# A long convolution by a two-stage Fourier transform: 2048 steps as 64 by 32 instead of 128 by 16, with half-array matmuls in the first and last stage

## The chip, the cores and the metric

One core of one Trainium2 chip. The metric is the device time of one execution in microseconds (us), over several executions; the profile is of one execution. A core has TensorE (PE; its weight loads are listed apart as PEld), VectorE (DVE), ScalarE (ACT), GpSimd (POOL) and SyncE (SP), each working through its own instructions in order, and 16 DMA engines which they start transfers on.

## The reference

Two branches over the same 2048 x 640 input `x`, joined at the end (bf16 inputs):

```python
x = A_q                                   # [1, 2048, 640]
xn = layernorm(x)
# branch A: q = xn
k_shift = sum(k_pad[:, t:t+S, :] * shift_k[:, 3-t] for t in range(4))
kv = k_shift * v
y = irfft(rfft(pad(kv, 2S)) * rfft(pad(ssm_k, 2S)))[:S]   # along the 2048 steps, per channel
s = xn * (y + kv * ssm_D)
# branch B
g = silu(gelu(xn @ w1 + b1) @ w2 + b2)    # 640 -> 1728 -> 640
out = x + s * g
```

## The kernel before

**The transform.** The convolution is done with real matmuls. The 2048 steps are numbered 16 p + j, with p = 0..127 on the partitions and j = 0..15 along the free axis (`NJ = 16`). The first stage contracts over the 128 partitions, for each j on its own: `k_f1` for the filter and `u_f1` for the gated input kv multiply a 128x128 matrix of cosines (`WA[:, j]`) and one of sines (`WB[:, j]`) with the 640 channels, in two halves of 320 (`HALF`). So one j is four matmuls of 128x128 weights with 320 columns, through `mm2` (L337). The results, of 128 lines each, are copied out of PSUM to bf16 (`evac`, ScalarE L135 or VectorE L136), stored to DRAM scratch (`k_store` L437, `u_store` L447, by GpSimd) and loaded again in another order by SyncE (`kin_load` L477, `uin_load` L513), which transposes between stages. The second stage (`k_f2`, `u_f2`) is one small 128x128 matrix for every group of lines. Its products with the filter's transform (`product`, L526 on VectorE) go through a first inverse stage (`inv1`, L534 and L535), again to scratch (`c_store` L541) and back (`cab_load` L547). The last stage `inv2` (L553, L554) adds, for each j, a cosine and a sine part: four matmuls of 128x128 weights (`GA`, `GB`) with 320 columns. `gate` (L560, VectorE) multiplies the result y with the rest, `out_add` (L564) adds x, and `out_store` (L568, GpSimd) or `last_store` (L416, SyncE) writes the output.

**Where the matrices come from.** `WA` and `WB` are made in the kernel: an integer product of step and frequency (L231 on VectorE, masked at L235), then three passes on ScalarE of 128x2048 (sine L239, absolute value L242, sine L244). `GA` and `GB` are their transposes, made on TensorE (`i2_tr` L488, 32 transposes in four steps it0 to it3). The filter comes with channels on the partitions, so it is transposed too: `k_tr` (L421), five 128x128 transposes per j.

**The second branch** is `ffn1` (L377, h: 128x512 matmuls, Gelu at L383) and `ffn2` (L396, g: groups of fourteen 128x320 matmuls, Silu at L401, product L406). The transposes of xn for it are tt (L368).

**PSUM** has a pool `big` of three buffers of two banks, for all of the transform, and a pool `ffn` of two buffers. A matmul that needs a buffer waits until its last user has read it.

**What sets the order.** A list written out by hand, `PLAN`, gives the order of all steps; the instructions of each engine stand in that order. A step such as `kf5` is one call of `k_f1(5)`, `ke5.a` copies its result out on ScalarE (`.d`: VectorE), `kt`, `kc` are the transposes of the filter and their copies, `uf`, `ue`, `us` the first stage of kv and its copies and stores, `y`, `yt`, `yo`, `ys` the last stage, its gate, add and store, `it`, `ie` the transposes of the matrices. The loads (`load_x` L168, `load_k` L173 to L175, `load_v` L179, `load_params` L187 to L191, `load_w1` L195, `xq_load` L544) are issued by SyncE in the order of the list. The first Gelu needs the bias b1, which is loaded by `load_params` and transposed on TensorE (`param_tr`, L505, 19 partitions).

Of the kernel before, what the change touches and what calls it, by code (L numbers as in the profile page):

```python
# [16 lines left out]
P = 128  # L17
# [16 lines left out]
ln7 ln5 ws2 C4 C3 C1 V0 cv7 cv15 C2 d kt0 kc0.a kt1 kc1.a kf0 kf1 ke0.a kt2 kc2.a V1 ln4 kf2 ke2.a cv24 cv23 X2  # L34
cv25 ke1.d ks0 gm2 ge4 ln6 kf3 ke3.d ks1 kf4 ke4.a gm4 ge5 kt3 kc3.d kf5 ke5.a ks2 V2 tt7 te7.a kt5 kc5.d tt9
te9.a kt4 gm5 kf7 cv26 cv27 cv28 kf6 kc4.a ke6.a ke7.a ks3 g6 ge6 kf8 ke8.a kf9 ke9.d ks4 kf10 ke10.a K2 tt8
te8.a kt6 kc6.d kf11 ke11.a ks5 kt9 kc9.d gm3 kf12 ke12.a tt5 te5.d tt6 te6.a uf1 kt7 kf13 kc7.a ke13.a ks6 g7
ge7 ls12 uf0 ue0.a ue1.d us0 cv29 cv30 cv31 V3 h14 he14 kf14 ke14.d kf15 ke15.d ks7 h15 he15 kt8 kc8.d kf19 kf18
ke18.a ke19.d ks9 kt10 kc10.a cv32 cv33 cv34 cv35 cv36 kf16 ke16.a kt12 cv40 kf17 kc12.a ke17.a ks8 h16 he16 uf3
uf2 ue2.a ue3.a us1 h17 he17 kf21 kf20 ke20.a ke21.d ks10 kt11 kc11.a h18 he18 uf5 uf4 ue4.a ue5.d us2 kf22  # L40
ke22.d ls10 h19 he19 kt14 kf24 ke24.d sm kf23 kc14.a ke23.a ks11 h20 he20 kf25 ke25.d ks12 kt13 kc13.d kf28
ke28.a h21 he21 uf6 ue6.a kf29 ke29.a ks14 uf7 ue7.a us3 h22 he22 h23 he23 kf26 ke26.a gm7 cv37 cv38 cv41 cv42
cv39 kf27 ke27.a ks13 kt15 kc15.d kf30 ke30.a kf31 ke31.a ks15 fl0 fl1 fl2 h24 he24 fl4 uf10 ue10.a gm6 ls15 ls8
ls9 uf8 ue8.a ls14 uf11 ue11.a us5 h25 he25 h26 he26 uf14 ue14.a cv43 ls13 lv3 lr3 h27 he27 cv44 ls11 lv2 lr2
cv45 cv46 cv47 uf12 ue12.a uf9 ue9.a us4 fl3 uf15 ue15.a us7 g8 ge8 gm8 ln13 ln9 uf13 ue13.a us6 fl5 g9 ge9 ff3
fe3.a ln12 ff1 fe1.d ln10 ff2 fe2.a cv56 ff0 fe0.a cv48 cv49 cv50 ln8 uf21 uf20 ue20.a ue21.a us10 ff8 fe8.a
ln11 g10 ge10 uf16 ue16.a ff6 fe6.d gm9 ff9 fe9.a fl7 ff5 fe5.a ff7 fe7.a fl9 ff4 fe4.a fl8 uf17 ue17.a us8 g11
ge11 cv51 cv52 cv53 cv54 cv55 ff11 fe11.a ff10 fe10.a fl6 uf18 ue18.d uf19 ue19.a us9 fl11 uf26 ue26.a cv57 cv58
cv59 uf24 ue24.a uf27 ue27.a us13 uf25 ue25.a us12 fl12 ff16 fe16.d ff17 fe17.a fl15 ff12 fe12.a tt12 te12.a
ff14 fe14.a cv60 cv61 cv62 cv63 ff18 fe18.a ff15 fe15.a fl13 g12 ff19 fe19.a fl10 uf22 ue22.d ff13 fe13.a fl14  # L50
uf31 gm11 ge12 uf30 ue30.a ue31.d us15 ff23 fe23.d gm12 uf23 ue23.a us11 gm10 tt14 te14.d uf29 uf28 ue28.d
ue29.a us14 mk0 ml0 ml1 mk1 mk2 mk3 ml2 ml3 ml5 ml4 ff31 fe31.a tt13 te13.a tt10 te10.d it0 ie0.d ff27 fe27.d
ff25 fe25.d g13 ge13 gm13 g14 ge14 gm14 ff29 fe29.d ln14 ff28 fe28.a ff24 fe24.d g15 ge15 gm15 ff21 fe21.a tt11
te11.d ff22 fe22.a mu0 mp0 ff26 fe26.a ml7 h28 he28 mu2 mp2 ml10 ml8 mu1 mp1 mk4 mc0 me0.a h29 he29 ff30 fe30.a
mu3 mp3 mk5 ml12 h30 he30 ml11 mc2 me2.a mu4 mp4 mc1 me1.a ms0 mu5 mp5 mk6 h31 he31 ml6 ff20 fe20.a mc3 me3.a
ms1 ln15 mu6 mp6 mc4 me4.a mu7 mp7 mk7 ml9 h32 he32 mu8 mp8 mc5 me5.a ms2 mc6 me6.a mu11 mp11 mc7 me7.a ms3 mu10
mp10 h33 he33 mu9 mp9 mk8 mk9 mc8 me8.a mc10 me10.a mu12 mp12 mu13 mp13 mk10 mc11 me11.a ms5 ml14 h34 he34 ml15
mc12 me12.a it1 ie1.d mc13 me13.a ms6 mu15 mp15 h35 he35 mu14 mp14 mk11 ml13 mc9 me9.a ms4 mu18 mp18 h36 he36
mc14 me14.a mu17 mp17 h37 he37 mu16 mp16 mk12 mc15 me15.a mu20 mp20 h38 he38 mu19 mp19 mk13 mc18 me18.a h39 he39
mu21 mp21 mk14 mc16 me16.a tt17 mc19 me19.a ms9 mc17 me17.a ms8 mu23 mp23 mc20 me20.a mu22 mp22 mk15 h40 he40  # L60
mc21 me21.a ms10 mu24 mp24 mu25 mp25 mc22 me22.a h41 he41 te17.d mc24 me24.a mu26 mp26 mc25 me25.a ms12 tt15
te15.a mu27 mp27 tt16 te16.d mc23 me23.a ms11 mc26 me26.a tt18 te18.d mu29 mp29 it3 ie3.a mu28 mp28 g16 ge16
gm16 mc27 me27.a ms13 it2 ie2.d tt19 te19.a mu31 mp31 mu30 mp30 ms7 q0 g17 ge17 gm17 mc28 me28.a mc31 mc29
me29.d ms14 mc30 me30.d me31.d ms15 yl5 yl2 yl0 yl4 yl3 yl1 yl6 yl11 yl15 q1 g18 ge18 gm18 g19 ge19 gm19 g20
ge20 gm20 g21 ge21 gm21 g22 ge22 gm22 g23 ge23 gm23 h42 he42 h43 he43 y0 yt0 yo0 h44 he44 h45 he45 h46 he46 y5
yt5 yl8 y4 yt4 yo4 yo5 ys2 y1 yt1 yo1 ys0 y3 yt3 h47 he47 h48 he48 h49 he49 h50 he50 h51 he51 y2 yt2 yl7 yl14
yl9 yl10 yl12 yo2 yo3 ys1 q2 h52 he52 h53 he53 h54 he54 h55 he55 y6 yt6 yl13 yo6 y7 yt7 yo7 ys3 q3 y8 yt8 yo8
y11 yt11 g24 ge24 g25 ge25 g26 y12 yt12 gm24 ge26 gm25 ga24 ga25 gs25 y15 yt15 g27 ge27 y14 yt14 y13 yt13 gm26
ga26 gm27 ga27 gs27 y9 yt9 yo9 ys4 y10 yt10 yo10 yo11 ys5 g28 ge28 gm28 ga28 g29 ge29 gm29 ga29 g30 ge30 gm30
ga30 gs30 g31 ge31 gm31 ga31 gs29 gs31  # L70
# [4 lines left out]
def kernel(  # L75
# [36 lines left out]
    x_v = A_q[0].rearrange("(p j) d -> p j d", j=NJ)  # L112
    k_v = A_k[0].rearrange("(p j) d -> p j d", j=NJ)
    v_v = A_v[0].rearrange("(p j) d -> p j d", j=NJ)
    out_v = out[0].rearrange("(p j) d -> p j d", j=NJ)
# [3 lines left out]
    scrC = dram.tile([P * 32, D], BF16, name="scrC")  # L119

# [31 lines left out]
    WA = consts.tile([P, NJ, P], BF16, name="WA")  # L152
    WB = consts.tile([P, NJ, P], BF16, name="WB")
    GA = consts.tile([P, NJ, P], BF16, name="GA")
    GB = consts.tile([P, NJ, P], BF16, name="GB")
# [9 lines left out]
    def load_x(c):  # L165
        for h in range(1 if c else 2):
            js = slice(2 * h, CH if c else 2 * h + 2)
            nc.sync.dma_start(out=xn_tiles[c][:, js, :], in_=x_v[:, c * CH:(c + 1) * CH, :][:, js, :])  # L168

    def load_k(i):  # L170
        r0 = i * KR
        if i == 0:
            nc.sync.dma_start(out=kh[16:P, 0:3, :], in_=k_v[15:P - 1, NJ - 3:NJ, :])  # L173
            nc.sync.dma_start(out=kh[1:16, 0:3, :], in_=k_v[0:15, NJ - 3:NJ, :])
        nc.sync.dma_start(out=kh[:, 3 + r0:3 + r0 + KR, :], in_=k_v[:, r0:r0 + KR, :])  # L175

    def load_v(i):
        r0 = i * KR
        nc.sync.dma_start(out=quad_of(("vc", i))[:], in_=v_v[:, r0:r0 + KR, :])  # L179

    kf_sb = Khat[:, 0:NG // 2, :].rearrange("p g d -> p (g d)").rearrange("p (t j) -> p t j", t=DT)
    kf_v = kf_sb.rearrange("p t (a b) -> p t b a", b=NJ)

    def load_params(i):
        with nc.allow_non_contiguous_dma(reason="tiny parameter loads"):
# [240 lines left out]
    def k_f1(i):  # L426
        mm2(big_of(("kf", i)), (WA, WB)[i % 2][:, i // 2, :], live["kT", i // 2])

# [278 lines left out]
```

## Time and profile before

| what | value |
|---|---|
| median of 3 runs | 229.34 us |
| runs | 227.24 to 229.63 us |
| span of the profiled execution, first to last instruction | 225.2 us |
| granted TensorE clock | 1.000 |
| DMA | 57.61 MB, mean 256 GB/s |

Some lines of the page's group table (line, engine, operation, out<-in, shape, count; then busy us, mean ns of one; then idle time before them and who ended it):

```profile
L377 PE MATMUL h<-xnT,w_sb 128*128 128x512 bf16 x280 | 65.8, 379 | 1.3 <-ACT hT L383 1.0
L396 PE MATMUL g<-w_sb,hT 128*128 128x320 bf16 x448 | 63.7, 299 | 0.6 <-ACT sl L401 0.6
L526 DVE TENSOR_TENSOR p<-mu,Khat 128x1280 bf16<-128x1280 f32 x32 | 45.8, 1484 | 3.1 <-PE mu L337 2.1
L383 ACT ACTIVATE hT<-h,b_f 128x512 bf16<-128x512 f32 (+1 forms) x56 | 38.3, 690 | 23.2 <-PE h L377 20.7
L337 PE MATMUL mu<-kh,mats 128*128 128x320 bf16 x64 | 13.6, 298 | 0.8 <-DMA kh<-scrU 0.4
```

`128*128` is partitions by weight columns, `128x320` the streamed operand. Matmuls are pipelined: the mean of one is its life from start to modelled end, and the next starts well before that end. The two matmul groups of the second branch (h and g) are the largest of TensorE, and they stand between the steps of the transform all through the kernel.

### The profile page before, as it was taken

Reading aid. Unit: us, or ns where it says so; the run is one execution under the profiler, and the core shown is the slowest. Engines: PE = TensorE matmul, PEld = TensorE weight load, DVE = VectorE, ACT = ScalarE, POOL = GpSimd, SP = SyncE. Lnnn points to the kernel's source line nnn. Section 1 sums busy time; section 2 is a strip of 40 time slices with the busy share of each in tenths; the row PEclk is TensorE's granted clock in tenths of the full one; section 3 lists DMA queues with packets and bytes.
Section 4 is the critical chain, followed back from the end, with each engine's and each line's share of the span. In section 5 each row is a group of like instructions: output and inputs, shape, how many; then the busy total and the mean of one; then the engine's idle time right before and its main releaser. Section 6 shows DMA issues by size and latency. Waiting matters only on the chain.

```text
span 225.2 us, 3912 instructions
## 1 busy us (share of the span) xinstructions
PE 209.3 (93%) x1420; PEld 131.5 (58%) x1420; DVE 183.2 (81%) x309; ACT 149.7 (66%) x232; POOL 42.5 (19%) x72
## 2 busy tenths in 40 slices
PE   7869989899999899979999988999999999999993
PEld 4624457677555556645765544565777755457771
DVE  7799999989989999999859998999996125445792
ACT  3946697998988999999549665576762263671111
POOL 8000011032232345030200221203222000100010
PEclk9999999999999999999999999999999999999999
DMA  6999996645844469599849999866833694389223
GB/s 215 347 381 357 406 410 277 218 193 198 303 186 189 178 209 388 185 320 324 320 167 286 335 399 361 273 231 254 273 118 140 215 367 153 119 260 388 80 92 116
DMA packets 25209, 57.61 MB, mean 256 GB/s; under 512 B 2854, under 2 KB 14055, under 8 KB 25190
## 3 DMA queue, kind: packets, MB, share of 16 engines
q1 hardware_dynamic: 20726, 39.66, 50.7%
q0 software_dynamic: 4320, 17.70, 20.6%
q8 instruction: 11, 0.18, 0.3%
q14 instruction: 8, 0.07, 0.1%
q10 hardware_dynamic: 144, 0.01, 0.0%
HBM read 33.76 MB, written 18.35 MB: 231 GB/s over the span
## 4 chain that ended last, share of the span: by engine, by line
PE 59%; issue 13%; ACT 11%; DVE 7%; DMA 7%; SPq 1%; POOL 1%; DVEq 0%; POOLq 0%; ACTq 0%
PE g L396 20%; PE h L377 20%; ACT Khat L135 5%; DMA prm<-in_B_b_dram 4%; PE uf L337 3%; PE mc L534 2%; DMA scrC<-c 2%; PE mc L535 2%; PE kf L337 2%; PE mu L337 2%; PE y L553 2%; PE y L554 2%; DVE p L526 2%; DVE Khat L136 2%; PE ff L337 1%
## 5 line engine op out<-in xcount | busy, mean ns | idle before, releaser
L377 PE MATMUL h<-xnT,w_sb 128*128 128x512 bf16 x280 | 65.8, 379 | 1.3 <-ACT hT L383 1.0
L396 PE MATMUL g<-w_sb,hT 128*128 128x320 bf16 x448 | 63.7, 299 | 0.6 <-ACT sl L401 0.6
L396 PEld LDWEIGHTS <-hT 128*128 128x128 bf16 x448 | 43.8, 98 | 18.1 <-issue 0.8
L383 ACT ACTIVATE hT<-h,b_f 128x512 bf16<-128x512 f32 (+1 forms) x56 | 38.3, 690 | 23.2 <-PE h L377 20.7
L526 DVE TENSOR_TENSOR p<-mu,Khat 128x1280 bf16<-128x1280 f32 x32 | 45.8, 1484 | 3.1 <-PE mu L337 2.1
L377 PEld LDWEIGHTS <-w_sb 128*128 128x128 bf16 x280 | 27.3, 98 | 29.3 <-issue 1.5
L401 ACT ACTIVATE sl<-g 128x320 bf16<-128x320 f32 x32 | 14.0, 439 | 36.1 <-PE g L396 32.5
L135 ACT CAST c<-mc 128x640 bf16<-128x640 f32 x29 | 19.9, 692 | 6.5 <-PE mc L535 5.7
L541 POOL DMA_DIRECT2D scrC<-c x16 | 11.5, 718 | 51.9 <-ACT c L135 47.7
L406 DVE TENSOR_TENSOR xn<-xn,sl 128x320 bf16<-128x320 bf16 x32 | 10.0, 320 | 13.7 <-ACT sl L401 13.5
L469 DVE TENSOR_TENSOR uc<-uc,kvtmp 128x1280 bf16<-128x1280 bf16 x24 | 19.8, 824 | 0.7
L473 DVE TENSOR_TENSOR kvtmp<-kh,w_exp 128x1280 bf16<-128x1280 bf16 x24 | 19.7, 819 | 0.5
L534 PE MATMUL mc<-p,mats 128*128 128x320 bf16 x64 | 18.1, 298 | 1.6 <-DVE p L526 1.1
L560 DVE TENSOR_TENSOR t<-y,xn 128x640 bf16<-128x640 f32 x12 | 9.8, 820 | 10.6 <-PE y L554 10.5
L337 PEld LDWEIGHTS <-mats 128*128 128x128 bf16 x128 | 12.0, 97 | 10.8 <-issue 3.8
L535 PE MATMUL mc<-p,mats 128*128 128x320 bf16 x64 | 18.1, 298 | 0.0
L135 ACT CAST Khat<-uf 128x640 bf16<-128x640 f32 x26 | 17.0, 697 | 0.4 <-PE uf L337 0.4
L135 ACT CAST Khat<-ff 128x640 bf16<-128x640 f32 x24 | 15.5, 699 | 0.5 <-PE ff L337 0.4
L135 ACT CAST Khat<-kf 128x640 bf16<-128x640 f32 x22 | 15.1, 711 | 0.3 <-PE kf L337 0.2
L437 POOL DMA_DIRECT2D scrK<-Khat x16 | 8.9, 554 | 29.7 <-ACT Khat L135 16.6
L337 PE MATMUL mu<-kh,mats 128*128 128x320 bf16 x64 | 13.6, 298 | 0.8 <-DMA kh<-scrU 0.4
L337 PE MATMUL ff<-kin,mats 128*128 128x320 bf16 x64 | 12.3, 298 | 1.3 <-ACT Khat L135 1.3
(111 smaller groups left out, 269.0 us busy)
## 6 DMA issues: line engine op xcount, KB each, us to landing
scrK<-Khat POOLq DMA_DIRECT2D x16, 320.0 KB, 2.5
scrU<-Khat POOLq DMA_DIRECT2D x16, 320.0 KB, 4.3
kin<-scrK SPq DMA_DIRECT2D x16, 320.0 KB, 4.9
Khat<-Khat SPq DMA_DIRECT2D x32, 160.0 KB, 3.8
kh<-scrU SPq DMA_DIRECT2D x16, 320.0 KB, 5.2
scrC<-c POOLq DMA_DIRECT2D x16, 320.0 KB, 3.6
kh<-scrC SPq DMA_DIRECT2D x16, 320.0 KB, 6.0
kh<-in_A_k_dram SPq DMA_DIRECT2D x4, 640.0 KB, 5.9
```

What stands on the lines that cost most here:

```text
L135: return nc.scalar.copy(out=out_ap, in_=in_ap)
L337: nc.tensor.matmul(out=ps[:, h, 0:HALF], lhsT=lhsT, rhs=rhs[:, h * HALF:(h + 1) * HALF], start=start, stop=stop)
L377: nc.tensor.matmul(out=ps[:, :], lhsT=w1_sb[:, t, ft * P:(ft + 1) * P], rhs=xnT[:, t, :], start=(t == 0), stop=(t == DT - 1))
L383: nc.scalar.activation(out=hT[0:M, ft, :], in_=live["h", i][0:M, :], func=ACT.Gelu_apprx_tanh, bias=b1_f[0:M, ft:ft + 1], scale=1.0)
L396: nc.tensor.matmul(out=ps[:, 0:HALF], lhsT=hT[0:M, ft, q * P:(q + 1) * P], rhs=w2_sb[0:M, ft, hs], start=(ft == 0), stop=(ft == FT - 1))
L401: nc.scalar.activation(out=sl[:], in_=live["g", i][:, 0:HALF], func=ACT.Silu)
L469: nc.vector.tensor_tensor(out=uc[:], in0=uc[:], in1=kvtmp[:], op=ALU.add)
L473: nc.vector.tensor_tensor(out=(kvtmp if s else uc)[:], in0=kh[:, r0:r0 + KC, :], in1=w_exp[:, j:j + 1, :].to_broadcast([P, KC, D]), op=ALU ...
L526: nc.vector.tensor_tensor(out=p[:].rearrange("p k (h c) -> p k h c", h=2), in0=live["mu", g][:, None, :, 0:HALF].to_broadcast([P, 2, 2, HA ...
L534: nc.tensor.matmul(out=psC[:, h, 0:HALF], lhsT=I1a, rhs=p[:, 0, hs], start=True, stop=False)
L535: nc.tensor.matmul(out=psC[:, h, 0:HALF], lhsT=I1b, rhs=p[:, 1, hs], start=False, stop=True)
L541: nc.gpsimd.dma_start(out=pair_view(scrC)[g2], in_=live["c", g2][:])
```

## The change

The steps are numbered 32 p + 16 a + j, with p = 0..63, a = 0 or 1 and j = 0..15: blocks of 16 steps, the even blocks (a = 0) on partitions 0 to 63, the odd blocks on 64 to 127. The first stage contracts over the 64 partitions of one side, for each j and a, and gives 64 frequencies, cosine and sine next to each other, in 128 output lines. So `WA` and `WB` become one matrix `W`, of which each side is half. `k_f1(j)` and `u_f1(j)` now do a whole j: four matmuls, each on 64 rows of the array, written in the order half 0 side 0, half 0 side 1, half 1 side 0, half 1 side 1, and into two big buffers (one for each a). `inv2` writes each side into its own 64 partitions of one buffer: four matmuls with 128 rows and 64 weight columns, with no accumulation. `k_tr` transposes 64 steps at a time, ten instead of five. The product and the three passes for the matrices are half as wide, and `i2_tr` runs twice instead of four times. The tile `spare` holds what `GB` lent as scratch space. The small matrices for the inner stages are made with three more small VectorE operations.

Every load or store of x, k, v and the output becomes two, one for each side (`in_sides`); the second has its issue right behind the first. In `PLAN` each pair `kf2i kf2i+1` becomes one step, mostly at the place of the second of them, `uf` likewise, and `it2`, `ie2`, `it3`, `ie3` go. All else stands in the same order.

```diff
-    x_v = A_q[0].rearrange("(p j) d -> p j d", j=NJ)
+    x_v = A_q[0].rearrange("(p a j) d -> a p j d", a=2, j=NJ)
...
+    def in_sides(eng, tile_ap, dram_ap, store=False):
+        for a in range(2):
+            s_ap, d_ap = tile_ap[a * 64:(a + 1) * 64], dram_ap[a]
+            eng.dma_start(out=d_ap if store else s_ap, in_=s_ap if store else d_ap)
...
-            nc.sync.dma_start(out=xn_tiles[c][:, js, :], in_=x_v[:, c * CH:(c + 1) * CH, :][:, js, :])
+            in_sides(nc.sync, xn_tiles[c][:, js, :], x_v[:, :, c * CH:(c + 1) * CH, :][:, :, js, :])
...
-            nc.scalar.activation(out=WB[:], in_=prod, func=ACT.Sin, scale=(2.0 * math.pi / L) * (1.0 - SIN_EPS),
+            nc.scalar.activation(out=W_c[:, :, 1, :], in_=prod, func=ACT.Sin, scale=(2.0 * math.pi / L) * (1.0 - SIN_EPS),
                                  bias=sin_bias[:])
...
         for t in range(DT):
-            nc.tensor.transpose(out=tp[:, t * P:(t + 1) * P], in_=kf_v[:, t, n2, :], identity=ident[:])
+            for a in range(2):
+                nc.tensor.transpose(out=tp[a * 64:(a + 1) * 64, t * P:(t + 1) * P], in_=kf_v[:, t, n2, a, :],
+                                    identity=ident[:])
...
+    def first_pair(name, j, rhs):
+        ps = [big_of((name, 2 * j + a)) for a in range(2)]
+        for h in range(2):
+            for a in range(2):
+                side = slice(a * 64, (a + 1) * 64)
+                nc.tensor.matmul(out=ps[a][:, h, 0:HALF], lhsT=W[side, j, :], rhs=rhs[side, h * HALF:(h + 1) * HALF],
+                                 start=True, stop=True)
+
     def k_f1(i):
-        mm2(big_of(("kf", i)), (WA, WB)[i % 2][:, i // 2, :], live["kT", i // 2])
+        first_pair("kf", i, live["kT", i])
...
     def u_f1(i):
-        n2 = i // 2
-        mm2(big_of(("uf", i)), (WA, WB)[i % 2][:, n2, :], live["uc", n2 // KC][:, n2 % KC, :])
+        first_pair("uf", i, live["uc", i // KC][:, i % KC, :])
...
-            nc.tensor.transpose(out=tp[:, q * P:(q + 1) * P], in_=(WA, WB)[i // 2][:, i % 2 * 8 + q, :], identity=ident[:])
+            nc.tensor.transpose(out=tp[:, q * P:(q + 1) * P], in_=W[:, i * 8 + q, :], identity=ident[:])
...
-            nc.tensor.matmul(out=psY[:, h, 0:HALF], lhsT=GA[:, n2, :], rhs=cab[:, 0, hs], start=True, stop=False)
-            nc.tensor.matmul(out=psY[:, h, 0:HALF], lhsT=GB[:, n2, :], rhs=cab[:, 1, hs], start=False, stop=True)
+            for a in range(2):
+                side = slice(a * 64, (a + 1) * 64)
+                nc.tensor.matmul(out=psY[side, h, 0:HALF], lhsT=G[:, n2, side], rhs=cab[:, a, hs], start=True, stop=True)
...
-        nc.gpsimd.dma_start(out=out_v[:, 2 * i:2 * i + 2, :], in_=live["o", i])
+        in_sides(nc.gpsimd, live["o", i], out_v[:, :, 2 * i:2 * i + 2, :], store=True)
```

One stretch of the list, before and after:

```diff
-h16 he16 uf3 uf2 ue2.a ue3.a us1 h17 he17 kf21 kf20 ke20.a ke21.d ks10 kt11 kc11.a
+h16 he16 uf1 ue2.a ue3.a us1 h17 he17 kf10 ke20.a ke21.d ks10 kt11 kc11.a
```

More of the change, by code (lines that the diff above doesn't have):

```diff
@@ L38 @@
[L38 to L42, printed above, removed]
@@ L203, in load_w2 @@
         nc.sync.dma_start(out=w2_sb[FLAST:FLAST + 1, FT - 1, :], in_=B_b2.rearrange("(o d) -> o d", o=1))
-    regions = [[t.rearrange("p a b -> p (a b)").bitcast(F32), 0] for t in (GB[:], GA[:], Khat[:, NG // 2:NG, :])]
+    regions = [[t.rearrange("p a b -> p (a b)").bitcast(F32), 0] for t in (spare[:], G[:], Khat[:, NG // 2:NG, :])]
     def scratch(shape, dtype):
@@ L243, in f1_sines @@
         else:
-            nc.scalar.activation(out=WA[:], in_=qabs, func=ACT.Sin, scale=2.0 * math.pi / L, bias=sin_bias_h[:])
+            nc.scalar.activation(out=W_c[:, :, 0, :], in_=qabs, func=ACT.Sin, scale=2.0 * math.pi / L, bias=sin_bias_h[:])
     sm = {}
@@ L415, in last_store @@
         hs = slice(0, D) if q < CH - 1 else hs
-        nc.sync.dma_start(out=out_v[:, c * CH + q, hs], in_=xn_tiles[c][:, q, hs])
+        in_sides(nc.sync, xn_tiles[c][:, q:q + 1, hs], out_v[:, :, c * CH + q:c * CH + q + 1, hs], store=True)
     def k_tr(n2):
```

142 lines of the change are left out of this document (78 added, 64 removed).

## The prediction

> **What bounds the kernel now.** I read the busy table, then the chain of waits, then busy time by stretch, then single groups, and last the timeline where one instruction follows the next.
>
> ```profile
> PE 209.3 (93%) x1420; PEld 131.5 (58%) x1420; DVE 183.2 (81%) x309; ACT 149.7 (66%) x232; POOL 42.5 (19%) x72
> ...
> PE 59%; issue 13%; ACT 11%; DVE 7%; DMA 7%; SPq 1%; POOL 1%; DVEq 0%; POOLq 0%; ACTq 0%
> ```
>
> TensorE is the busiest engine and holds 59% of the chain, but the average mixes two kinds of stage. Busy time by stretch (PE, PEld, DVE, ACT, POOL, then clock, DMA share, GB/s):
>
> ```profile
> 41.00:109.00 68.00, 63.29 (x458) 40.97 (x457) 64.69 (x115) 63.46 (x106) 20.13 (x33) 1.00 0.70 249
> 184.00:214.00 30.00, 30.00 (x186) 17.98 (x184) 16.31 (x28) 12.65 (x20) 2.19 (x4) 1.00 0.59 213
> ```
>
> From 41 to 109 us, where the first stages kf and uf run, VectorE (64.7 of 68) and ScalarE (63.5) are as full as TensorE. From 184 to 214 us, where the last stage y runs, TensorE alone is full. The clock is 1.00, so nothing is gained or lost there.
>
> Groups that the change touches (busy us, mean ns of one):
>
> ```profile
> L337 PE MATMUL kf<-kT,WA 128*128 128x320 bf16 x32 | 7.0, 299 | 1.7 <-DVE kT L136 0.7 <-ACT kT L135 0.6 <-ACT Khat L135 0.2
> L337 PE MATMUL uf<-uc,WB 128*128 128x320 bf16 x32 | 6.7, 298 | 1.0 <-ACT Khat L135 0.7 <-DVE Khat L136 0.3
> L553 PE MATMUL y<-kh,GA 128*128 128x320 bf16 x32 | 8.9, 299 | 0.0
> L421 PE MATMUL kt<-ident,Khat 128*128 128x128 bf16 x80 | 7.4, 225 | 0.4 <-ACT Khat L135 0.2
> ```
>
> The 299 ns is the life of one matmul, not its price. The price is the distance between starts, which the timeline gives (start, length, engine):
>
> ```profile
> 202.71 5.88 PE L396 MATMUL g<-w_sb,hT 128*128 128x320 bf16 x42
> ...
> 10.53 0.72 PE L305 MATMUL psw<-ident,skp 128*128 128x64 bf16 x10
> ```
>
> 42 matmuls of 320 columns: (5.88 - 0.30) / 41 = 0.136 us each. Ten of 64 columns, each with its own load of 128 weight columns: (0.72 - 0.25) / 9 = 0.053 us, not a fifth of 0.136 as the columns would have it. So a load of 128 weight columns costs at least 0.053 to 0.055, whatever streams behind it. In the transposes (128 columns) 0.055 (tt) to 0.062 (kt) is the step. Summing price by count over 41 to 109 us (h 70 x 0.216, g 99, ff 44, kf 64 and uf 64 at 0.136, kt 80 x 0.06, tt 36 x 0.055) gives 58.7 of 68: TensorE really has some 9 us to spare there, most of it in waits for an evacuation.
>
> **The first stage (kf, uf).** Per step j there are four matmuls before and four after, each after on half of the rows, two at a time. Before: 4 x 0.136 = 0.54. After, if halves run beside each other: in the trace a weight load starts with the matmul ahead of it and is worth 0.055, so the second half starts 0.055 behind the first; the second pair starts 0.136 after the first; the group lasts 0.055 + 2 x 0.136 = 0.325. Saved 0.215 x 32 steps = 6.9 us of TensorE. No row shows two half-array matmuls, so the ends are 0 (one after the other) and 8.7 (perfectly paired). [...]
>
> **The transposes kt.** 80 become 160, each with 64 weight columns and 128 streamed. Ends per group of ten: 0.28 (pairs side by side) and 0.60 (each 0.06 as now), against 0.30 now. I take the middle, 0.45, because the psw row says that the load of weights can set the step and nothing says what 64 columns cost: +0.15 x 16 = +2.4 (-0.3 to +4.8).
>
> **Changes of array form.** In the order of the built instructions TensorE changes between the 128x128, 64x128 and 128x64 forms 67 times up to the end of the first stage and 12 times in the last. The kernel before has one stretch of another form, the transpose of the parameters on 19 partitions. I compare the weight load behind it with one inside a plain run:
>
> ```profile
> 14.61 0.09 PEld L505 LDWEIGHTS <-prm 19*128 19x128 bf16 x1 [1.22 <-DMA prm<-in_B_b_dram]
> 14.64 0.17 PE L505 MATMUL pt<-ident,prm 19*128 19x19 bf16 x1 [0.76 <-DMA prm<-in_B_b_dram]
> 14.73 0.10 PEld L377 LDWEIGHTS <-w_sb 128*128 128x128 bf16 x1
> ...
> 208.43 0.30 PE L553 MATMUL y<-kh,GA 128*128 128x320 bf16 x1
> 208.43 0.10 PEld L554 LDWEIGHTS <-GB 128*128 128x128 bf16 x1
> ```
>
> In the plain run the next load starts with the matmul; behind the change of form it starts 0.09 later, though 19 columns are long through. So a change seems to hold the next load 0.09 behind the stream, and the load itself (0.055) is then uncovered: 0.14 each. Ends: 0 (that gap was dispatch) and 0.22 (the tail of a matmul, 0.299 - 0.136 = 0.163, plus the load). One row is thin evidence, but it is the only one of its kind, so I take 0.14. [...]
>
> First stage, sum on TensorE: 67 x 0.14 = +9.4, -6.9, +2.4: +4.9 us. TensorE has 9 to spare by price, but its waits are tied to evacuations that run in order behind it, and VectorE has 3.3 idle: I let half reach the end, +2.4 (0 to +4.9).
>
> **The last stage (y).** In the order, y comes as 1, 4, 1, 4, 2, 4 steps between other work. A step falls from 0.54 to 0.325. Single steps save 0.215 each (four: 0.9). Runs of four hit the three big PSUM buffers: the fourth waits for the gate (L560) of the first.
>
> ```profile
> 188.11 0.30 PE L553 MATMUL y<-kh,GA 128*128 128x320 bf16 x1
> ...
> 188.85 1.55 DVE L560 TENSOR_TENSOR t<-y,xn 128x640 bf16<-128x640 f32 x2 [2.43 <-PE y L554]
> ```
>
> The gate starts 0.20 after the step's last start-to-start (188.11 + 0.54) and takes 0.82; after, the fourth step starts at 0.325 + 0.20 + 0.82 = 1.35 and ends at 1.68 instead of 2.16: 0.48 saved, twice, and some 0.1 in the last run of four, where VectorE is already behind. Together 1.9. Twelve changes of form take 1.7 back: -0.2.
>
> **The rest.** The transposes of the inverse matrix (it) fall from 32 to 16; the two that vanish stood at 162.4 and 165.6 us in full TensorE: 16 x 0.055 = -0.9. The three sines halve (2.0 each, ScalarE -3.0) and product and phase too (VectorE, -1.7): TensorE runs unbroken from 33.35 to 41.1 us and the copy kT starts at 41.62 behind the last sine, so only some 0.3 of it is on the path: -0.3. Three more small VectorE operations (0.15 each) run before 15 us where ScalarE waits for the parameters: nothing; without that cover 0.45. Loads of x, k, v and x again and all stores split in two. A half load moves at the queue's full rate (160 KB in a 0.42 us issue is 380 GB/s, what the engines move there), so only the start suffers: SyncE issues three more transfers ahead of the parameters (L189, L187),
>
> ```profile
> 4.39 9.65 DMA prm<-in_B_b_dram
> ```
>
> which already wait 9.65 us in full queues, with ScalarE's first Gelu and the h matmuls behind them: +0.3 (0 to 3 x 0.42 = 1.3). SyncE's other extra issues (16 more of 0.33 to 0.44) stand where it waits on blocked queues or on VectorE. The six POOL stores become twelve at 0.55 on an engine 19% busy, which waits 40.8 us for what it stores: nothing. The last store is two issues behind one another: +0.4 with nothing to cover it.
>
> **Sum:** +2.4 - 0.2 - 0.9 - 0.3 + 0.3 + 0.4 = +1.7 on the span of 225.2, so 226.9. The median of the runs is 229.34, 4.1 above that span (launch and end); I add the same: 231.0 us.
>
> **Rivals.** *Changes of form are free* (the gap at 14.64 was dispatch): the first stage sheds 4.5 to 6.9 of TensorE but VectorE has only 3.3 idle, and its own row order keeps most, so -1.0; y -1.9; it -0.9; the rest +0.4: -3.4, 225.9. For it: transposes and plain matmuls already follow each other without a gap (kf at 45.32, two matmuls, then tt at 45.59: 0.27 = 2 x 0.136). Against: the 0.09. It decides when a change costs under some 0.08. *Halves do not overlap*: kf and uf stay at 0.54, kt +4.8, 67 x 0.14: +14.2 against 9 spare, of which two thirds shows: +9.5; y +1.7, the rest -0.5: 240. That is also the case in which the change doesn't do what it says. Against it stands only that the built order names separate halves and separate PSUM banks. [...] *Two buffers at once*: a step now needs two of three big buffers together, and h and g are queued behind it on TensorE; if a fill (0.325 + 0.16) is uncovered in one step of five, 32 x 0.49 / 5 = +3.1 on ScalarE and VectorE, which have no room: 234. The page's releasers put only 2.3 us of kf's and uf's waits on evacuations, which speaks for a small share.
>
> **Chances.** Forecast 0.48 (faster, same, slower 0.03, 0.20, 0.25: its costs reach from 229 to 237 with the switch at 0.22: 14.7 - 6.9 + 2.4 = 10.2, three quarters 7.6, y +0.7, rest -0.5, so +7.8). Free changes 0.30 (0.23, 0.06, 0.01). No overlap 0.13 (slower). Two buffers 0.09 (0.01, 0.02, 0.06). Together faster 0.27, same 0.28, slower 0.45, where 1% (2.3 us) is about what a measurement of this kernel can tell from no change. The range runs from just under the free case, 225.5, to the dear switch, 237, and leaves out most of the case without overlap.
>
> **What would show it.** In the changed profile: two kf matmuls of one step starting 0.055 apart (or 0.136: no overlap); the distance from the last start of a kf group to the next plain matmul, 0.136 + 0.14 (or 0.136: free); ten kt in 0.45; the step from y to y in a run of four; TensorE's idle before kf naming ScalarE's Khat (two buffers); the first h behind the parameters at 15.8 + 0.3. The forecast falls if the switch distance is under 0.05 or over 0.2, or if the stretch up to the last uf (109 us) moves by more than 3 us either way.

## The result, and the profile after

The changed kernel takes 257.45 us (median of 4 runs, 255.76 to 258.53) where the kernel before takes 229.49 on the same chip: a ratio of 1.126, with an interval of 1.118 to 1.134. The forecast was 231.0, with a range to 237.0. The profiled execution spans 256.4 us, at a granted clock of 0.938 where it was 1.000. Each ratio below is to the kernel before on the same chip; the profiled executions of late_whole, full_single and full_kt5_single took 1.6 to 2.8 per cent longer than the fastest one of their kernel, so of these three only times and counts are used.

The busy table, and from the chain of waits the shares by engine (the chain could be followed back only to 107.8 us, so its shares add up to 55 per cent of the span):

```profile
PE 217.6 (85%) x1471; PEld 126.7 (49%) x1484; DVE 182.1 (71%) x315; ACT 147.9 (58%) x231; POOL 46.3 (18%) x81
...
PE 43%; ACT 5%; DVE 3%; DMA 3%; issue 1%; SPq 0%; DVEq 0%
```

VectorE and ScalarE are busy for as long as before (183.2 and 149.7) in a longer span. Nothing has become the bound; all engines wait more. Where, is read from the starts of the first and last instructions of some groups in the two traces (us):

| stretch | before | after | difference |
|---|---|---|---|
| start to first kf | 42.35 | 58.70 | +16.4 |
| first kf to last uf (first stage) | 65.6 | 76.7 | +11.2 |
| last uf to first mu | 9.6 | 10.8 | +1.3 |
| first mu to first y | 66.8 | 64.9 | -2.0 |
| first y to the end | 40.9 | 45.2 | +4.3 |
| span | 225.2 | 256.4 | +31.1 |

More than half is lost before the first stage begins, in a part where the change touches no arithmetic but some small operations. Busy time by stretch of the kernel after (PE, PEld, DVE, ACT, POOL, then clock, DMA share, GB/s):

```profile
15.00:30.00 15.00, 10.64 (x38) 4.28 (x37) 10.56 (x18) 4.70 (x7) 0.00 (x0) 0.77 1.07 276
...
45.00:60.00 15.00, 6.83 (x64) 4.68 (x61) 7.25 (x13) 5.10 (x7) 0.00 (x0) 0.79 1.04 220
60.00:75.00 15.00, 13.46 (x132) 8.77 (x129) 10.45 (x21) 11.06 (x20) 3.45 (x6) 0.76 0.63 201
```

and of the kernel before, in the same view:

```profile
15.00:30.00 15.00, 14.21 (x70) 6.80 (x70) 14.52 (x23) 9.88 (x15) 0.00 (x0) 1.00 1.04 381
```

From 15 to 30 us the DMA engines are as full as before (share 1.07 against 1.04) and move 276 GB/s instead of 381; from 45 to 60 us they are still full (1.04), at 220. The columns of the engines fall: TensorE, VectorE and ScalarE wait for data. The packets take longer: in the trace's DMA records between 15 and 30 us the median packet of 5120 B takes 408 ns, against 201 before. TensorE's clock is low behind these stretches, too: 0.76 from 60 to 75 us, where the DMA share is down to 0.63. The parameters are transposed at 19.88 us, and the first h behind them, forecast at 15.8 + 0.3, starts at 21.04:

```profile
19.88 0.17 PE L531 MATMUL pt<-ident,prm 19*128 19x19 bf16 x1 [3.33 <-DMA prm<-in_B_b_dram]
21.04 3.57 PE L395 MATMUL h<-xnT,w_sb 128*128 128x512 bf16 x8 [0.98 <-ACT hT L401]
```

Time is lost at the end too, where x is loaded again for the last gate. This piece of the chain that ended last was not on it before:

```profile
230.64 8.08 DMA xq<-in_A_q_dram
```

By itself it doesn't show what the halves cost: with whole loads (experiment 1) this load lies on the chain as well, with 6.79 us. Experiment 6 measures it.

The half-array matmuls themselves do what the change says. TensorE's timeline around one step of uf and one of kt (start, length):

```profile
88.32 0.81 PE L395 MATMUL h<-xnT,w_sb 128*128 128x512 bf16 x3
89.06 0.45 PE L451 MATMUL uf<-uc,W 64*128 64x320 bf16 x4
89.44 1.25 PE L395 MATMUL h<-xnT,w_sb 128*128 128x512 bf16 x5
90.62 0.77 PE L440 MATMUL kt<-ident,Khat 128*64 128x128 bf16 x10
```

and the weight loads behind it:

```profile
89.06 0.11 PEld L451 LDWEIGHTS <-W 64*128 64x128 bf16 x4 [0.42 <-issue]
...
90.62 0.63 PEld L440 LDWEIGHTS <-Khat 128*64 128x64 bf16 x10 [0.42 <-issue]
```

Four uf matmuls take 0.45 us from the first start to the last end. With a life of 0.30 the last starts 0.15 after the first, where four of 128 rows start over 0.41. The single records say 89.060 and 89.063 for one pair, 89.205 and 89.209 for the next. The four weight loads lie within 0.11 us. The next h starts at 89.437: 0.136 for the last pair to stream, and 0.09 for the change of form, since plain matmuls of this length follow each other by 0.136 in both traces. The ten transposes start in pairs, the second pair 0.16 behind the first and the others 0.11 apart (90.620, 90.780, 90.890, 91.001, 91.114). With 0.11 for the last pair they take 0.60, against 0.30 for the five of before.

### The profile page after: what moved, and what is told of

Same layout as the page of the kernel before. It is cut to its first block, busy times and chain, and to the rows that moved or that the text cites. A ratio compares the mean times of both kernels' runs of the same rounds, so it can differ in the third digit from the quotient of the medians.

```text
span 256.4 us, 4081 instructions
## 1 busy us (share of the span) xinstructions
PE 217.6 (85%) x1471; PEld 126.7 (49%) x1484; DVE 182.1 (71%) x315; ACT 147.9 (58%) x231; POOL 46.3 (18%) x81
## 4 chain that ended last, share of the span: by engine, by line
PE 43%; ACT 5%; DVE 3%; DMA 3%; issue 1%; SPq 0%; DVEq 0%
PE g L414 16%; PE h L395 11%; ACT Khat L138 4%; PE mc L560 4%; DMA xq<-in_A_q_dram 3%; PE mc L561 3%; PE mu L355 3%; PE ff L355 3%; PE uf L451 1%; PE y L581 1%; DVE p L552 1%; DVE t L587 1%; ACT c L138 1%; PE tt L386 1%; DVE xn L587 1%
## 5 line engine op out<-in xcount | busy, mean ns | idle before, releaser
L414 PE MATMUL g<-w_sb,hT 128*128 128x320 bf16 x448 | 65.7, 304 | 1.0 <-ACT sl L419 1.0
L440 PE MATMUL kt<-ident,Khat 128*64 128x128 bf16 x160 | 12.3, 297 | 8.4 <-DVE Khat L521 7.6
L355 PEld LDWEIGHTS <-mats 128*128 128x128 bf16 x128 | 12.6, 101 | 11.4 <-issue 5.3
L138 ACT CAST Khat<-uf 128x640 bf16<-128x640 f32 x26 | 16.9, 701 | 1.5 <-PE uf L451 1.0
L440 PEld LDWEIGHTS <-Khat 128*64 128x64 bf16 x160 | 10.7, 201 | 12.2 <-DVE Khat L521 7.9
```

Source lines behind the costliest of these rows:

```text
L138: return nc.scalar.copy(out=out_ap, in_=in_ap)
L355: nc.tensor.matmul(out=ps[:, h, 0:HALF], lhsT=lhsT, rhs=rhs[:, h * HALF:(h + 1) * HALF], start=start, stop=stop)
L414: nc.tensor.matmul(out=ps[:, 0:HALF], lhsT=hT[0:M, ft, q * P:(q + 1) * P], rhs=w2_sb[0:M, ft, hs], start=(ft == 0), stop=(ft == FT - 1))
L440: nc.tensor.transpose(out=tp[a * 64:(a + 1) * 64, t * P:(t + 1) * P], in_=kf_v[:, t, n2, a, :], identity=ident[:])
```

## The experiments

The first question is the transfers. The change alters two things about them: each touches 64 adjacent partitions instead of 128, from blocks that lie 40960 B apart in DRAM, and there are twice as many. The rivals sit in the first stage: two buffers of PSUM at once, the transposes in halves, the changes of form. "Whole loads" below means that a load or store is one transfer of 128 partitions in the natural order of the steps, so that the other steps than the reference's lie on the two halves; all instructions on the engines stay as they are.

**1. Whole loads in the kernel after (full_loads).**

```diff
-    x_v = A_q[0].rearrange("(p a j) d -> a p j d", a=2, j=NJ)
+    x_v = A_q[0].rearrange("(o p j) d -> o p j d", o=1, j=NJ)
...
-        for a in range(2):
-            s_ap, d_ap = tile_ap[a * 64:(a + 1) * 64], dram_ap[a]
-            eng.dma_start(out=d_ap if store else s_ap, in_=s_ap if store else d_ap)
+        d_ap = dram_ap[0]
+        eng.dma_start(out=d_ap if store else tile_ap, in_=tile_ap if store else d_ap)
```

> The changed kernel, but every load and store of x, k, v and the output is one transfer over all 128 partitions again, with the steps laid out as before; so the halves hold other steps than the transform wants and the output is not the reference's, while every matmul, copy and wait stays. Theory A (a transfer that lands on 64 adjacent partitions moves at half the rate, and nearly all of the loss is that): the first kf matmul comes back from 58.7 to 42 to 45 us and the time to 229 to 236 us. Rival B (the changes of array form and the half-array transposes cost most of it): it stays above 245 us.

Measured: 236.13 us, ratio 1.041 (1.030 to 1.052), against 1.126: the transfers cost 8.5 per cent, 19.5 us. The packets are back at 202 ns, and in the view by stretch so is the rate:

```profile
15.00:30.00 15.00, 13.77 (x57) 6.01 (x58) 14.52 (x24) 8.50 (x13) 0.00 (x0) 0.89 1.04 381
```

The first kf comes at 44.40 instead of 58.70 and the end 40.0 instead of 45.2 after the first y: 14.3 + 5.2 = 19.5 us, so the trace finds what the ratio says. What stays is 4.1 per cent, most of it in the first stage (73.7 us against 65.6).

**2. and 3. Halves in the kernel before, of adjacent and of alternate partitions (before_halves, before_evenodd).** The kernel before with each transfer cut in two, once into partitions 0 to 63 and 64 to 127, once into the even and the odd ones. The second has the spacing in DRAM of the change and the same number of transfers, but each of its halves reaches over all 128 partitions.

```diff
+    def in_parts(eng, tile_ap, dram_ap, store=False):
+        for a in range(2):
+            s_ap, d_ap = tile_ap[a * 64:(a + 1) * 64], dram_ap[a * 64:(a + 1) * 64]
+            eng.dma_start(out=d_ap if store else s_ap, in_=s_ap if store else d_ap)
```

with `[a:P:2]` for the slices in the second.

> The kernel before, with each load and store of x, k, v and the output cut into partitions 0 to 63 and 64 to 127; the source of each half is one solid block of steps. Theory A (the half of the partitions is what is slow): 245 to 255 us, packets of 5120 B at some 400 ns instead of 202. Rival C (the source in blocks 40960 B apart is slow): 229 to 232 us. Rival D (twice the number of transfers is slow): 245 us or more as well.

> The kernel before, with each of those transfers cut into the even and the odd partitions; the source of each has blocks 40960 B apart, as in the changed kernel, and there are as many transfers as there. Theory A: 229 to 233 us, packets of 5120 B at 200 to 215 ns. Rivals C (source spacing) and D (number of transfers): 245 us or more.

Measured: 247.80 us, ratio 1.088 (1.077 to 1.099), for adjacent partitions, and 233.47 us, 1.026 (1.017 to 1.036), for alternate ones. By stretch, first the adjacent, then the alternate halves:

```profile
15.00:30.00 15.00, 12.04 (x46) 4.97 (x45) 9.98 (x14) 5.53 (x9) 0.00 (x0) 0.82 1.07 280
```

```profile
15.00:30.00 15.00, 11.89 (x48) 4.99 (x48) 11.75 (x16) 6.76 (x10) 0.00 (x0) 0.89 1.05 377
```

280 GB/s against 377, with median packets of 385 ns against 201. So it is the adjacency in the memory of the core, not the spacing in DRAM. A packet takes nearly twice the time for adjacent halves, and no more for alternate ones; what lies behind that, no run shows. The number of transfers, together with the spacing in DRAM, costs 2.6 per cent: with alternate halves VectorE copies the bias at 17.83 us (14.84 before), behind a queue with more issues ahead of the parameters. So some 6 of the 8.8 per cent are the rate.

**4. The second halves on other queues (two_queues).** The second half of each load is issued by ScalarE (x, k and half of v) or GpSimd (the rest of v, and xq).

```diff
-            eng.dma_start(out=d_ap if store else s_ap, in_=s_ap if store else d_ap)
+            (other if a and other else eng).dma_start(out=d_ap if store else s_ap, in_=s_ap if store else d_ap)
```

> The changed kernel, with the second half of each load issued from another engine than SyncE: x, k and the first two of v from ScalarE, the last two of v and the second load of x from GpSimd. Theory A, if halves in flight together fill both sides: the first kf at 44 to 50 us, 232 to 245 us. Rival E (the 16 engines take one half after the other whatever the queue): 252 to 260 us.

Measured: 273.13 us, ratio 1.201 (1.189 to 1.213). This decides little: ScalarE's issues wait behind its own work, so that the DMA engines move nothing from 54 to 61 us, and VectorE waits 16.9 us for k. While both queues are at work (15 to 60 us) their median packets take 386 and 353 ns, so another queue is at least no quick remedy.

**5. One transfer for both halves (one_transfer).** The arithmetic and the numbering of the change, with a whole tile against the even blocks followed by the odd ones:

```diff
-        for a in range(2):
-            s_ap, d_ap = tile_ap[a * 64:(a + 1) * 64], dram_ap[a]
-            eng.dma_start(out=d_ap if store else s_ap, in_=s_ap if store else d_ap)
+        if store:
+            eng.dma_start(out=dram_ap, in_=tile_ap)
+        else:
+            eng.dma_start(out=tile_ap, in_=dram_ap)
```

> The changed kernel with all its arithmetic and its numbering of the steps, but each load or store of x, k, v and the output is one transfer: the whole tile of 128 partitions against the even blocks followed by the odd blocks in DRAM. Theory (transfers that touch 64 adjacent partitions are slow and twice as many): as the run with whole loads, ratio 1.04 (1.03 to 1.05, 236 us), packets of 5120 B back near 202 ns. Rival (the blocks, 40960 B apart in DRAM, cost as such when 128 of them are in one transfer, or the transfer is cut in two inside): between 1.06 and 1.126, packets above 250 ns.

Measured: 398.59 us, ratio 1.752 (1.741 to 1.764). Both expectations missed. A stretch in which only such loads run:

```profile
105.00:110.00 5.00, 0.00 (x0) 0.00 (x0) 0.00 (x0) 0.00 (x0) 0.00 (x0) 0.50 0.13 52
```

The packets are fast (202 ns), but the share is 0.13, that is 2 of 16 engines, and 2 x 5120 B / 202 ns = 51 GB/s is the rate shown. The outermost step of the transfer in DRAM has two values here, as many as engines are at work; that the one sets the other is the author's reading, and no run with another number of blocks tests it. A second run of the kind, with one big buffer at a time and the integer work of the small matrices moved (one_transfer_single), had the same fault and its time, 399.24 us (1.753), tells nothing of its other edits.

> The run above, with the first stage as in the order of before (one side and one big buffer at a time, two half-array matmuls each) and the four steps of s (small matrices' integer work) moved behind the copy of the parameters. The transposes kt stay in halves. If the parts add up (two buffers at once 2.9, the start 1.7): 236 - 4.6 = 231.4, ratio about 1.01 (1.00 to 1.02). If the start is not due to s, or the single order was worth less than one disturbed run made it look: 1.025 to 1.04.

**6. Only the late transfers whole (late_whole).** In the kernel after, the second load of x and the output's stores are whole; x, k and v stay in halves.

```diff
-        in_sides(nc.sync, quad_of(("xq", c))[:], x_v[:, :, c * CH:(c + 1) * CH, :])
+        nc.sync.dma_start(out=quad_of(("xq", c))[:], in_=xw_v[:, c * CH:(c + 1) * CH, :])
```

> The changed kernel, halves kept for the loads of x, k and v, but the second load of x (xq) and all stores of the output in whole transfers of 128 partitions in the natural order of the steps (so the x that is added and the places written are those of other steps). Theory: the part from the first y to the end falls from 45.2 to about 41, the wait of VectorE's w_exp for xq (5.2) goes, time 253, ratio 1.105 (1.095 to 1.115). Rival (the late end follows from the early part alone, as everything behind it): y to end stays at 44 to 45 and the ratio at 1.12 to 1.13.

Measured: 250.16 us, ratio 1.097 (1.087 to 1.107). The late halves cost 2.9 of the 8.5 per cent, some 6.7 us; the early ones the other 5.6 per cent. The trace of experiment 1 put the same two parts at 5.2 and 14.3 us.

**7. Two big buffers at once, without halves (before_pairs).** The kernel before, with both outputs of a j as one step, at its place in the order of the kernel after; all matmuls over 128 rows.

```diff
     def k_f1(i):
-        mm2(big_of(("kf", i)), (WA, WB)[i % 2][:, i // 2, :], live["kT", i // 2])
+        ps = [big_of(("kf", 2 * i + a)) for a in range(2)]
+        for a in range(2):
+            mm2(ps[a], (WA, WB)[a][:, i, :], live["kT", i])
```

> The kernel before, whole-array matmuls and whole transfers, but its first stage in the order of the changed kernel: both outputs of a step j at once, two big PSUM buffers together. Theory F (the rest of the loss, some 9 us with whole loads, is the changes of array form and the slower transposes): no change, 226 to 229 us. Rival P (it is the two buffers at once): 231 to 236 us.

Measured: 232.47 us, ratio 1.021 (1.014 to 1.027); the first stage takes 71.2 us instead of 65.6. The waits of the copies and of uf (who waited, for whom: us in total, times, longest), first of this kernel:

```profile
DVE Khat L134 <- PE uf L335: 4.0, 3, 1.8
...
PE uf L335 <- ACT Khat L133: 2.4, 8, 0.5
```

then of the kernel before:

```profile
PE uf L337 <- ACT Khat L135: 1.0, 5, 0.3
DVE Khat L136 <- PE uf L337: 0.8, 2, 0.6
```

A step that must hold two of three buffers waits for the copies of the last one, and then the copies wait for it. With whole loads in the kernel after, the wait of uf for the copies is larger still:

```profile
PE uf L450 <- ACT Khat L137: 3.9, 9, 0.8
```

Not all of the 5.6 us is waiting. In the trace of before_pairs the clock is at half for 3.4 us within the first stage, which costs at most 1.7 us and makes the longest kf matmul 471 ns, against 309 before. By stretch (columns as above):

```profile
61.97:65.39 3.42, 3.38 (x11) 1.43 (x10) 3.32 (x6) 2.35 (x4) 0.92 (x2) 0.50 0.59 237
```

Three executions of each kernel have a mean clock of 0.990 to 0.993. They took 232.4 us on average here and 228.9 in the kernel before, so some 3.5 us remain at an equal clock.

**8. The transposes whole again (full_kt5).** Whole loads, and five transposes of 128x128 per step in the natural order.

```diff
-            for a in range(2):
-                nc.tensor.transpose(out=tp[a * 64:(a + 1) * 64, t * P:(t + 1) * P], in_=kf_v[:, t, n2, a, :],
-                                    identity=ident[:])
+            nc.tensor.transpose(out=tp[:, t * P:(t + 1) * P], in_=kf_v[:, t, n2, :], identity=ident[:])
```

> full_loads with the filter's transposes as five whole-array transposes per step again (in the order of the steps, so what stands on the partitions is not what the transform wants): 11 fewer changes of form in the first stage and 16 times some 0.25 us less. Against full_loads with 236.1 us: theory F 230.5 to 233 us; rival P 235 to 237 us.

Measured: 233.98 us, ratio 1.025 (1.021 to 1.029), against 1.041: the half transposes, with the 11 changes of form that go with them (58 left of 69), cost 1.5 per cent, 3.5 us. The result lies between the two expectations, and the intervals leave 0.3 to 2.7 per cent.

**9. The first stage over all rows (full_plain).** The run above, with the four matmuls of a step over 128 rows, which mixes even and odd blocks: no overlap, and no change of form before y.

```diff
-                nc.tensor.matmul(out=ps[a][:, h, 0:HALF], lhsT=W[side, j, :], rhs=rhs[side, h * HALF:(h + 1) * HALF],
+                nc.tensor.matmul(out=ps[a][:, h, 0:HALF], lhsT=W[:, j, :], rhs=rhs[:, h * HALF:(h + 1) * HALF],
```

> full_kt5 with the first stage's matmuls over all 128 rows too, four per step and still two buffers at once (another sum than the transform's). No change of form before the last stage. Theory F: 226 to 229 us, the sines and the transposes it saved, y a little cheaper. Rival P: 231 to 236 us. If pairs of half-array matmuls are worth their changes of form, it is slower than full_kt5.

Measured: 233.68 us, ratio 1.023 (1.018 to 1.029): the same as with halves, and in the range of rival P. What the pairs save on TensorE does not reach the end. The changes of form that they bring can have taken it back, and so can the clock: it was 0.968 to 0.976 in the executions with halves and 0.984 to 0.991 here, and no run holds it equal.

**10. One big buffer at a time (full_single).** Whole loads, the half transposes, and the first stage in the order of before: one side of a j, two matmuls, one buffer.

```diff
-    def first_pair(name, j, rhs):
-        ps = [big_of((name, 2 * j + a)) for a in range(2)]
...
+    def first_half(name, i, rhs):
+        j, a = divmod(i, 2)
+        side = slice(a * 64, (a + 1) * 64)
+        mm2(big_of((name, i)), W[side, j, :], rhs[side, :])
```

> full_loads with the first stage in the order of the kernel before: each half of a step on its own, two half-array matmuls and one big buffer, so two halves run beside each other only where they stand next to each other. Theory F: 236 to 240 us, since there are 11 more changes of form and less overlap. Rival P: 230 to 233 us.

Measured: 235.13 us, ratio 1.028 (1.022 to 1.034), against 1.041: better by 1.3 per cent, which lies between the two expectations and at the edge of the intervals, although the sides of a step run less beside each other and TensorE changes form 80 times instead of 69 by the trace's records.

**11. Both together, and then without forms (full_kt5_single, full_plain_single).** The edits of 8 and 10 in one kernel, and this with the edit of 9. The last has before's first stage in all but the matrix, and keeps the change's gains: half the product and sines, 16 transposes it, the paired y.

> Whole loads and stores, five whole-array transposes kt per step in natural order, and the first stage in the order of before with one side and one big buffer at a time (half-array matmuls of other steps than the reference's). If the parts add up: 236.1 - 3.5 (transposes) - 2.9 (two buffers at once) = 229.7 us, ratio 1.012 (1.003 to 1.020). Rival (both take away the same waits for big buffers, so that only one of them counts): 1.022 to 1.030.

> The run above, with the first stage over all 128 rows (both sides of W together, which mixes the even and odd blocks), so that there is no change of array form before the last stage: the first stage is that of before, and only the gains of the change (sines, product, it, y) and its start remain. Theory: first stage 65 to 67 us long as in before (65.6), time 227.5 to 229, ratio 0.997 to 1.006: forms without pairs cost about 1 per cent in the run above. Rival (changes of form cost nothing on the path): within 0.3 per cent of the run above.

Measured: 230.54 us, ratio 1.0125 (1.006 to 1.019), and 226.32 us, 0.994 (0.990 to 0.998, 10 runs). The parts add up, as the first theory had it. The second run is 1.8 per cent below the first, and below its theory's range: with little of the overlap of pairs, some 70 changes of form cost up to 4.2 us on the path. Part of that goes with the clock, which was 0.975 to 0.992 in the executions of the first and 0.990 to 1.000 in those of the second. One stretch of 3.4 us at half clock, which takes 0.0075 off the mean, costs some 1.6 us: on this chip the kernel before took 227.1 us on average in nine executions with 0.997 to 1.000, and 228.7 in four with 0.992. At 0.990 to 0.992 the two kernels took 229.1 us (one execution) and 227.2 us (five), so nearer 2 us are left at an equal clock. Why the clock falls more often with half-array matmuls is not shown. The first stage of the second run takes 66.05 us, as before (65.6). Against full_plain (1.023), which differs only in taking two buffers at once, it is 2.9 per cent faster: the clearest measure of what that costs, the clock (0.984 to 0.991 there) included. Since its first stage mixes the blocks, it measures the gains and replaces neither kernel. Of the runs that keep the change's half-array first stage and half transposes, the best (full_single, with whole loads, which the layout can't use) is still 2.8 per cent above the kernel before.

**12. The small matrices' integer work moved (full_start).** In all runs with whole loads the first kf is still 1.7 us or more late. In full_loads VectorE copies the bias at 15.25 us, 0.81 after the transpose pt; before it came 0.20 after it. The chain of small operations stands ahead of it. It has more new ones than the three named above: 15 operations on 128x1 elements instead of 8, and it takes 4.36 us instead of 3.51. So the step `s` was moved behind the copy.

```diff
-em K0 sp s A0 h0 h1 P2 ee.a A1 P1 P0 pt pb he0
+em K0 sp A0 h0 h1 P2 ee.a A1 P1 P0 pt pb s he0
```

> The run with whole loads, with only s moved behind pb (the integer work on VectorE behind the copy of b_f instead of ahead of it). Theory: the copy of b_f falls back to 14.8 us (15.25), TensorE does not idle there long enough for its clock to drop, first kf at 42.4 to 42.9 (44.4), time 234.3, ratio 1.032. Rival (the late start comes from the load order or from slower transfers): first kf stays at 44 or later and the ratio at 1.04.

Measured: 240.79 us, ratio 1.058 (1.049 to 1.066): worse, and neither expectation. The copy does follow pt at once, as hoped:

```profile
15.55 0.17 DVE L534 CAST b_f<-pt 128x14 f32<-128x14 bf16 x1 [4.12 <-PE pt L530]
```

But VectorE idles 4.12 us for it, and does the 4 us of integer work afterwards, ahead of the convolution of k: the first kf moves from 44.40 to 46.61. `s` had filled a hole. The rest of the loss lies in the first stage (76.2 us instead of 73.7), where the clock was at half from 48.0 to 54.8 us. In this profile the parameters themselves came 0.9 us later (pt at 15.35), so the edit wasn't tested under equal conditions at the start. What goes with the late start is seen on TensorE. The kernel before, then full_loads, from 14 us on:

```profile
14.64 0.17 PE L505 MATMUL pt<-ident,prm 19*128 19x19 bf16 x1 [0.76 <-DMA prm<-in_B_b_dram]
15.79 5.56 PE L377 MATMUL h<-xnT,w_sb 128*128 128x512 bf16 x25 [0.98 <-ACT hT L383]
```

```profile
14.44 0.17 PE L530 MATMUL pt<-ident,prm 19*128 19x19 bf16 x1 [0.88 <-DMA prm<-in_B_b_dram]
16.18 5.00 PE L394 MATMUL h<-xnT,w_sb 128*128 128x512 bf16 x16 [1.58 <-ACT hT L400]
```

and full_loads by stretch:

```profile
15.00:20.00 5.00, 3.82 (x12) 1.46 (x12) 4.93 (x9) 2.02 (x4) 0.00 (x0) 0.66 1.07 363
```

The clock falls to half for 3.4 us (15.6 to 19.0): 16 matmuls of h in 5.00 us where 25 took 5.56. Half speed for 3.4 us is 1.7 us, nearly all of the late start. The longer wait behind the transpose is not shown to be the cause, though: when the clock fell, TensorE had idled 0.88 and 1.0 us, hardly more than the 0.76 and 0.98 of before, and the rest of the 1.58 came afterwards. In the clock records of before and after each level holds for 3.41 us or a whole multiple of it (from 5.87 us of after on: 13.65, 6.83, 27.31, 13.65 us). In the 3.41 us that ended with the fall TensorE was busy for 1.46 us; in those of the kernel before that contain the same transpose (13.82 to 17.23 us, counted back in steps of 3.41 us from the change at 225.44) for 1.67, and its clock stayed. What decides, the idle time or the moment, is not shown. Whether the small operations alone would bring it about wasn't tried.

## Why the prediction was wrong

The shares, in per cent of the kernel before, each from two runs that differ in one edit: transfers in halves 8.5 (1.126 to 1.041), half transposes 1.5 (to 1.025), two buffers at once less what pairs save 1.3 (to 1.0125), changes of form without pairs 1.8 (to 0.994), and -0.6 for the gains less the late start. Together they make the 12.6 of the result by construction. Each holds what the clock lost with it, and the three small ones are known to about 1 per cent each.

- **The step that failed** is "A half load moves at the queue's full rate (160 KB in a 0.42 us issue is 380 GB/s, what the engines move there), so only the start suffers": +0.3 in the sum, 19.5 us measured. The 380 GB/s was the rate of transfers over all 128 partitions; no row of before shows one over 64 adjacent ones, so the row bounded nothing. The dependence on DMA was visible: a share of 1.02 to 1.07 from 5 to 35 us means that every loss of rate there is a loss of time. SyncE issues some 5.9 MB of x, k and v in the first 29 us; half of 381 GB/s for them is 15 us more, and that end belonged in the range. The start was too small as well: alternate halves, whose packets are as fast as whole ones (201 ns), cost the kernel before 2.6 per cent, some 6 us, where the extra issues ahead of the parameters had +0.3 (0 to 1.3).
- **The last loads and stores** were costed at 0.4 us (two issues of the last store) and nothing for the rest. The second load of x came to lie on the chain, with 8.08 us of waiting; the late halves cost 6.7 by experiment 6.
- **Halves overlap**: right, and better than forecast. A step takes 0.28 (0.145 + 0.136), not 0.325, and saves 8.3 us of TensorE instead of 6.9. The starts of a pair lie mostly 3 to 6 ns apart in the trace of after, where the forecast had 0.055 us.
- **Changes of form**: the direction was right, the size 0.14 too high. The timeline of after gives 0.09 to 0.096 (from h to uf 0.312 instead of 0.216, from uf to h 0.226 instead of 0.136), so 67 of them are 6.4 us, not 9.4.
- **Transposes**: 0.60 for ten, not 0.45, which is the upper of the bounds (0.28 to 0.60): +4.8 instead of +2.4 on TensorE. On the path they and their 11 changes of form cost 3.5.
- **First stage**: on TensorE the three prices sum to 6.4 - 8.3 + 4.8 = +2.9, less than the +4.9 forecast. Yet with whole loads the stage grew by 8.1 us, not by 2.4. Prices on TensorE were the wrong account for it. In a stage where three engines are full, the third of the rivals weighs most: *two buffers at once*, given +3.1 and a chance of 0.09. By itself it costs 5.6 us of the stage and 2.1 per cent, 4.7 us, of the whole (before_pairs; 3.5 us at an equal clock). The argument against it, that the page names only 2.3 us of waits for evacuations, looked at a kernel in which a step never asked for two.
- **Last stage**: steps in a run follow each other by 0.27 instead of 0.54, and the twelve changes of form take part of it back: a net -0.2 was forecast. With whole loads the first y stands 40.0 us before the end, against 40.9, so the part is somewhat better than that. **it**: the stretch from mu to y falls by 2.0 us, of which the forecast had 0.9; no run separates the rest.
- **Three small VectorE operations**, "nothing", or 0.45 without cover: there are seven more, 0.85 us, and VectorE did run late for the copy behind them. The first kf is 1.7 to 2.4 us late in the traces of experiments 1, 8, 9 and 11, for which a stretch at half clock (some 1.7 us) could account. Why the clock falls there is open (experiment 12).
- **The 4.1 us for launch and end** took a median of several executions against the span of one. In every later run the time is 1.7 to 1.9 us above the span of the same execution; the rest was scatter. It does not touch the forecast of +1.7.

Of the list of what would make the forecast fall, the stretch up to the last uf (135.43 us, not 109) says it at once, and the reading of h behind the parameters (21.04 us, not 16.1) names the place.

## What to carry to other kernels

The layout that puts halves of the data on halves of the partitions was paid for by its transfers, with 19.5 us. So look at the DMA share of the stretch that feeds such a layout first (1.04 here before the change), and price a transfer by the partitions and the outermost step that it covers, not by its bytes: a packet of 5120 B took 385 and 408 ns over 64 adjacent partitions against 201, and loads with two outermost blocks ran at 52 GB/s. Where a row of the profile does not contain the shape that the change introduces, its rate is no price but one end of a range. And a matmul made cheaper by taking two outputs at once earned nothing here (233.98 us with pairs, 233.68 without), where the three buffers behind it are emptied one at a time.

## What the hardware showed

- Loads over 64 adjacent partitions had median packets (5120 B, 15 to 30 us) of 385 and 408 ns (before_halves, after), loads over 64 alternate or 128 partitions 201 ns (before_evenodd, before). Those with two outermost blocks in DRAM ran at a DMA share of 0.13, that is 2 of 16 engines, and 52 GB/s (one_transfer).
- Matmuls on the two row halves, and on the two column halves, mostly started 3 to 6 ns apart in the trace of after, their weight loads mostly 3 or 4. A change of form cost TensorE 0.09 to 0.096 us. Weight loads of 64 columns for the transposes took longer than those of 128 (201 ns on average against 147 in before), and pairs of them followed 0.11 us apart:

```profile
L440 PEld LDWEIGHTS <-Khat 128*64 128x64 bf16 x160 | 10.7, 201 | 12.2 <-DVE Khat L521 7.9 <-issue 3.7 <-PE h L395 0.3
```

- In its records TensorE's clock held each level for 3.41 us or a whole multiple of it: 218.45 us in before, and 13.65, 6.83, 27.31, 13.65, 58.03, 3.41, 6.83, 3.41, 102.40, 3.41 and 10.24 us in after. It fell to half at the end of 3.41 us with 1.46 us busy (full_loads) and stayed after 3.41 us with 1.67 (before), but busy time alone does not tell the cases apart: at 118.0 us in full_loads it fell after 3.41 us with 2.40. Executions of the kernel before at a mean clock of 0.992, as one stretch of 3.4 us at half makes it, took 1.6 us more than those at 0.997 to 1.000 (228.7 against 227.1 us).
